# Splitting the attention burst between slots 8, 9 and 10, 11 of a fused retention and bilinear feed-forward kernel

## The chip, the cores and the metric

One core of a Trainium2 chip runs the whole program in one launch. The metric is the device time in microseconds (us). The engines are named as in the profile: PE (TensorE, its weight loads as PEld), DVE (VectorE), ACT (ScalarE), POOL (GpSimd) and SP (SyncE, which here issues all DMAs).

## The reference

A recurrent linear attention with a decay for each head feeds a bilinear feed-forward layer:

```python
# q, k, v: [4 batches, 8 heads, 768 steps, 64]
for t in range(S):
    state = gamma[None, :, None, None] * state + np.einsum('bhd,bhe->bhde', k[:, :, t], v[:, :, t])
    y[:, :, t] = scale * np.einsum('bhd,bhde->bhe', q[:, :, t], state)
x = y.transpose(0, 2, 1, 3).reshape(3072, 512)
out = ((x @ w_a) * (x @ w_b)) @ w_out        # w_a, w_b: 512 x 1536, w_out: 1536 x 512
```

## The kernel before

**Slots.** The 3072 tokens are cut into 24 slots of 128 tokens, six to a batch; slots 6 to 11 are the second batch. Two neighbouring slots form a pair. For each slot, q and k are multiplied by tables of the decay and cast to bf16 (`scaled`, tile `kqb`), then turned so that the head dimension lies on partitions (`kqT`). For the first three pairs the turning is done by PE (`flip2`: transposes into a PSUM tile `tp`, then one copy by ACT for k and one by DVE for q). For all later slots it is a DMA transpose, which `casts(t)` issues on SP right after POOL has made `kqb`; behind it, still in `casts(t)`, SP issues the loads of slot t+2.

**Attention of a slot.** `scores` multiplies k by q into two PSUM tiles `at` (32 small matmuls, line 261) and DVE multiplies them by a causal mask into `aT` (line 267). `update` adds k times v to the running state `st` in PSUM (8 matmuls, line 278) and copies it to `gst`, on the engine that it is given. `inter` multiplies q by `gst` (line 298) and `intra` multiplies `aT` by v (line 308), both into `ys`; `leave` copies `ys` to `xt`, the input of the feed-forward layer, on ACT.

**Bursts.** `turn(new, old, eng)` puts these together: scores and updates of the pair that begins at slot `new`, then `inter`, `intra` and `leave` of the pair that begins at `old`; either may be `None`. For `new` = 10 the last slot of the batch needs no update, so `turn` makes one update alone, that of slot 10: behind `inter` where there is an old pair, ahead of the scores where there is none.

**Feed-forward.** The slots are taken in eight groups J of `TILES` = 4, 2, 2, 2, 2, 4, 4, 4 slots. Group 2 holds slots 6 and 7, group 3 slots 8 and 9. `ffn_ab(J, ft)` is one of twelve steps of a group: four matmuls `a` (line 449), a cast of them by ACT (line 452), four matmuls `g` (line 459), and a product of both by DVE into `ht` (line 461). In groups 1 to 4 a matmul has 256 columns, in the others 512. The product with w_out is made for group 0 directly (`ffn_out`), for the others by a scheme of seven products of half matrices (`Group`, line 546) that uses sums of parts of `ht` (tiles `hs`, `hsum` and `hsums`, made by POOL for groups 2 to 4). `single(J, ...)` mixes these seven products with the first three steps of the next group.

**PSUM.** The eight banks are `ff` (three, in turn for `a`, `g`, `o`, `tp` and, with `scores(t, True)`, the two `at` tiles of one slot), `at0`, `at1`, `y0`, `y1` (one each) and `st`.

**Order.** Nothing is reordered on an engine: `seq` chains every instruction to the one before it on its engine, so the order of the calls at the end of the kernel (lines 620 to 794) is the order on every engine and on SP's queue. The part around the change:

```python
    turn(8, None)          # line 728: scores of 8 and 9, and their updates
    blocks(2, 7, 9)
    hsums(2, 0, 3, G_)
    casts(12)
    blocks(2, 9, 10)
    turn(10, 8, V_)        # line 733
    blocks(2, 10, NFT)
    hsums(2, 3, 6, G_)
    casts(13)
    single(2, Y0, AT0, FF)
    casts(14)
    blocks(3, 3, 6)
```

Of the kernel before, what the change touches and what calls it, by code (L numbers as in the profile page):

```python
# [10 lines left out]
BF16 = mybir.dt.bfloat16  # L11
# [12 lines left out]
def kernel(  # L24
# [11 lines left out]
    P = 128  # L36
    B, H, S, D = q.shape
    NCH = S // P
    HP = H // 2
# [24 lines left out]
    psff = ctx.enter_context(tc.tile_pool(name="psff", bufs=3, space=bass.MemoryType.PSUM))  # L64
    psat = ctx.enter_context(tc.tile_pool(name="psat", bufs=1, space=bass.MemoryType.PSUM))
# [6 lines left out]
    def seq(bi):  # L72
        ins = bi.ins
        prev = last.get(ins.engine)
        if prev is not None:
            tc.add_manual_dep(ins, prev.name, nosync, reason="program order")
        last[ins.engine] = ins
        return bi
# [114 lines left out]
    def cast(engine, dst, src):  # L193
        if engine is nc.scalar:
            seq(nc.scalar.copy(dst, src))
        else:
            seq(engine.tensor_copy(dst, src))  # L197
# [38 lines left out]
    def casts(t):  # L236
        new_nat(t)
        scaled(nc.gpsimd, t, 0)
        scaled(nc.gpsimd, t, 1)
        if t not in range(12, 20):  # L240
            cast(nc.gpsimd, vb[t], raws["v", t])
        if t % 2 == 0:
            kqT[t // 2] = tra.tile([P, 2, 2, HP, P], BF16, tag="kqT", name="kqT", bufs=3)
        seq(nc.sync.dma_start_transpose(
            out=kqT[t // 2][:, t % 2].rearrange("p a b c -> p (a b) c"),
            in_=kqb[t].rearrange("p a hp r d -> p (a hp r d)")))
        if t + 2 < NSLOT:
            load_slot(t + 2)
# [4 lines left out]
    def scores(t, ff):  # L253
        if ff:
            at = [psff.tile([P, HP, P], F32, tag="ff", name=f"at{r}") for r in range(2)]
        else:
            at = [psat.tile([P, HP, P], F32, tag=f"at{r}", name="at") for r in range(2)]
        for hp in range(HP):
            for c in range(2):
                for r in range(2):  # L260
                    seq(nc.tensor.matmul(at[r][half(c), hp, :],  # L261
                                         kqT[t // 2][half(r), t % 2, 0, hp, half(c)],
                                         kqT[t // 2][half(r), :, 1, hp, half(t % 2)],
                                         start=True, stop=True, skip_group_check=True))
        aT[t] = tra.tile([P, 2, HP, P], BF16, tag="aT", name="aT")
        for r in range(2):
            seq(nc.vector.tensor_tensor(aT[t][:, r], at[r], mask.to_broadcast([P, HP, P]), op=ALU.mult))  # L267

    def update(t, eng):
        ci = t % NCH  # L270
        if ci == NCH - 1:
            return
        if ci == 0:
            state[0] = psst.tile([P, HP, D], F32, tag="st", name="st")
        st = state[0]
        for hp in range(HP):
            for r in range(2):
                seq(nc.tensor.matmul(st[half(r), hp, :], kb[t][:, hp, r, :],  # L278
                                     vb[t][:, HP * r + hp, :],
                                     start=(ci == 0 and hp == 0), stop=(hp == HP - 1),  # L280
                                     skip_group_check=True))
        cast(eng, gst[(t + 1) % 4], st)
# [8 lines left out]
    def inter(t):  # L291
        if t % NCH == 0:
            return
        for j in range(2):
            for c in range(2):
                for r in range(2):
                    hp = 2 * j + c
                    seq(nc.tensor.matmul(ys[t // 2][r][half(c), j, :, t % 2, :],  # L298
                                         gst[t % 4][half(r), hp, :],
                                         kqT[t // 2][half(r), :, 1, hp, half(t % 2)],  # L300
                                         start=begin(t, c, r), stop=False, skip_group_check=True))

    def intra(t):
        for r in range(2):
            for j in range(2):
                for c in range(2):
                    hp = 2 * j + c
                    seq(nc.tensor.matmul(ys[t // 2][r][half(c), j, :, t % 2, :],  # L308
                                         vb[t][:, HP * r + hp, :], aT[t][:, r, hp, :],
                                         start=begin(t, c, r), stop=True, skip_group_check=True))  # L310

    def leave(t):
        J, i = where[t]
        if i == 0:
            xt[J] = xtp.tile([P, KT, 4 * P], BF16, tag="xt", name="xt")
        for r in range(2):
            seq(nc.scalar.copy(xt[J][:, 2 * r : 2 * r + 2, i * P : (i + 2) * P],  # L317
                               ys[t // 2][r].rearrange("p j a s n -> p j (a s n)")))

    def turn(new, old, eng=nc.scalar):  # L320
        if old is not None:
            ys[old // 2] = [psat.tile([P, 2, 2, 2, P // 2], F32, tag=f"y{r}", name="y") for r in range(2)]
        two = new is not None and (new + 1) % NCH < NCH - 1
        if new is not None:
            if two or old is None:
                update(new, eng)
            scores(new + 1, True)
            scores(new, False)
        if old is not None:
            inter(old)  # L330
            inter(old + 1)
        if two:
            update(new + 1, nc.scalar)
        elif new is not None and old is not None:
            update(new, eng)
        if old is not None:
            intra(old)
            intra(old + 1)
            leave(old)
# [9 lines left out]
        for t in (2 * u, 2 * u + 1):  # L349
            cast(nc.gpsimd, vb[t], raws["v", t])  # L350

    def flip2(u, i, on):
        if i == 0:
            kqT2[u] = tra.tile([P, 2, 2, HP, P], BF16, tag="kqT2", name="kqT2", bufs=2)
        for pars, eng in on:
            tp = psff.tile([P, 2, HP, P], BF16, tag="ff", name="tp")[:, : len(pars)]
            for n, par in enumerate(pars):
                for hp in range(HP):
                    seq(nc.tensor.transpose(tp[:, n, hp, :], kqb[2 * u + par][:, i, hp, :, :], ident))  # L359
            cast(eng, kqT2[u][:, pars[0] : pars[0] + len(pars), i], tp)  # L360
# [81 lines left out]
    def ffn_a(J, ft, c0=0, c1=None):  # L442
        c1 = TILES[J] * P if c1 is None else c1
        if J not in ht:
            ht[J] = htp.tile([P, NFT, 4 * P], BF16, tag="ht", name="ht")
        fs = slice(ft * P, (ft + 1) * P)
        a = psff.tile([P, 4 * P], F32, tag="ff", name="a")[:, : c1 - c0]
        for kt in range(KT):
            seq(nc.tensor.matmul(a, wa_bf[:, kt, fs], xcols(J, kt, c0, c1),  # L449
                                 start=(kt == 0), stop=(kt == KT - 1)))  # L450
        asb = asbs[J, ft, c0] = asbp.tile([P, 4 * P], BF16, tag="asb", name="asb")[:, : c1 - c0]
        seq(nc.scalar.copy(asb, a))  # L452

    def ffn_g(J, ft, c0=0, c1=None):
        c1 = TILES[J] * P if c1 is None else c1
        fs = slice(ft * P, (ft + 1) * P)
        g = psff.tile([P, 4 * P], F32, tag="ff", name="g")[:, : c1 - c0]
        for kt in range(KT):
            seq(nc.tensor.matmul(g, wb_bf[:, kt, fs], xcols(J, kt, c0, c1),  # L459
                                 start=(kt == 0), stop=(kt == KT - 1)))  # L460
        seq(nc.vector.tensor_tensor(ht[J][:, ft, c0:c1], g, asbs.pop((J, ft, c0)), op=ALU.mult))  # L461

    def ffn_ab(J, ft):
        store()
        ffn_a(J, ft)
        ffn_g(J, ft)
# [56 lines left out]
    def sums(J, ft):  # L523
        for what in WHEN.get(ft, []):
            hsum(J, *map(int, what))
# [94 lines left out]
    D_, G_, A_ = nc.vector, nc.gpsimd, nc.scalar  # L620
    K, Q = 0, 1
    warm(psat, "y1", 512, 512, 256)
    casts2(0, {(K, 1): D_, (K, 0): D_, (Q, 1): D_, (Q, 0): D_})
    flip2(0, K, [((0, 1), A_)])
    warm(psat, "y1", 128)
    flip2(0, Q, [((1,), D_)])
    flip2(0, Q, [((0,), D_)])
    warm(psat, "y1", 256)
    scores2(0, 1)
# [43 lines left out]
            scaled(D_, 5, Q)  # L673
    flip2(2, K, [((0, 1), A_)])
    ffn_a(0, 9)
    flip2(2, Q, [((0, 1), D_)])
    ffn_g(0, 9)
    scores2(2, 0, True)
    scores2(2, 1)
# [11 lines left out]
    V_ = nc.vector  # L691

    def blocks(J, a, b):
        for ft in range(a, b):
            ffn_ab(J, ft)
            if J >= 5:
                sums(J, ft)
# [32 lines left out]
    hsums(2, 0, 3, G_)  # L730
    casts(12)
    blocks(2, 9, 10)
    turn(10, 8, V_)
    blocks(2, 10, NFT)
    hsums(2, 3, 6, G_)
    casts(13)
    single(2, Y0, AT0, FF)
    casts(14)
    blocks(3, 3, 6)
    hsum(3, 3, 0, 6, G_)  # L740
    v_cast(12)
    blocks(3, 6, 8)
# [82 lines left out]
```

## Time and profile before

| | |
|---|---|
| time of the kernel, 3 runs | median 228.40 us (228.40 to 228.43) |
| the profiled execution | 228.36 us, its span 226.4 us, granted TensorE clock 0.998 |
| PE, DVE, ACT, POOL busy | 96%, 57%, 41%, 42% of the span |
| DMA | 39.67 MB, 74.4% of 16 engines |

In a timeline row the first number is the start, the second the duration, both in us from the start of the span; `[1.68 <-DMA x]` means that the engine stood idle for 1.68 us before the row until the DMA that writes x had landed. A PE row runs to the modelled end of its last matmul, which reaches into the next row: what a row costs in a full stream is the distance of the starts. In a row of waits stand the sum, the number of times and the longest.

### The profile page before, as it was taken

Reading aid. Unit: us, or ns where it says so; the run is one execution under the profiler, and the core shown is the slowest. Engines: PE = TensorE matmul, PEld = TensorE weight load, DVE = VectorE, ACT = ScalarE, POOL = GpSimd, SP = SyncE. Lnnn points to the kernel's source line nnn. Section 1 sums busy time; section 2 is a strip of 40 time slices with the busy share of each in tenths; the row PEclk is TensorE's granted clock in tenths of the full one; section 3 lists DMA queues with packets and bytes.
Section 4 is the critical chain, followed back from the end, with each engine's and each line's share of the span. In section 5 each row is a group of like instructions: output and inputs, shape, how many; then the busy total and the mean of one; then the engine's idle time right before and its main releaser. Section 6 shows DMA issues by size and latency. Waiting matters only on the chain.

```text
span 226.4 us, 5592 instructions
## 1 busy us (share of the span) xinstructions
PE 217.7 (96%) x2253; PEld 146.5 (65%) x2264; DVE 129.5 (57%) x255; ACT 91.9 (41%) x202; POOL 94.0 (42%) x111
## 2 busy tenths in 40 slices
PE   7899999999999969999999999999999999999993
PEld 3567445687468858888888555468654468444582
DVE  3785338646983565455476337993366563346732
ACT  3364334342243424464565355353343433333331
POOL 5365666677653767669629846600000000000000
PEclk9999999999999999999999999999999999999999
DMA  6999999999999997999897999920400000400005
GB/s 166 290 326 349 346 289 335 387 250 188 256 257 234 209 222 182 194 250 214 182 198 181 223 194 232 230 53 3 185 3 0 1 3 8 178 3 0 0 1 184
DMA packets 86904, 39.67 MB, mean 175 GB/s; under 512 B 57440, under 2 KB 82528, under 8 KB 86880
## 3 DMA queue, kind: packets, MB, share of 16 engines
q1 hardware_dynamic: 86880, 39.33, 74.4%
q8 instruction: 17, 0.28, 0.5%
q14 instruction: 7, 0.06, 0.1%
HBM read 28.31 MB, written 6.29 MB: 153 GB/s over the span
## 4 chain that ended last, share of the span: by engine, by line
PE 88%; DMA 6%; DVE 2%; SPq 2%; issue 1%; POOL 0%; DVEq 0%; POOLq 0%
PE g L459 27%; PE a L449 27%; PE mA L546 12%; PE mB L546 6%; PE o L480 5%; DMA qf<-in_q_dram 3%; PE mC L546 3%; DMA kqT<-kqb 2%; PE at L261 2%; PE y L308 2%; SPq L99 2%; PE st L278 1%; DVE kqb L229 1%; PE y L298 1%; PE y L414 1%; PE tp L359 1%
## 5 line engine op out<-in xcount | busy, mean ns | idle before, releaser
L461 DVE TENSOR_TENSOR ht<-g,asb 128x256 bf16<-128x256 f32 (+1 forms) x98 | 53.7, 549 | 55.6 <-PE g L459 50.8
L459 PE MATMUL g<-xt,wb_bf 128*128 128x256 bf16 (+1 forms) x392 | 77.8, 322 | 0.1
L449 PE MATMUL a<-xt,wa_bf 128*128 128x256 bf16 (+1 forms) x383 | 77.4, 321 | 0.5
L452 ACT CAST asb<-a 128x256 bf16<-128x256 f32 (+1 forms) x98 | 46.3, 473 | 67.1 <-PE a L449 64.7
L459 PEld LDWEIGHTS <-wb_bf 128*128 128x128 bf16 x392 | 38.2, 98 | 24.0
L449 PEld LDWEIGHTS <-wa_bf 128*128 128x128 bf16 x392 | 37.3, 98 | 22.4 <-issue 0.4
L229 POOL TENSOR_TENSOR kqb<-kf,ktab 128x512 bf16<-128x512 f32 x22 | 23.3, 1064 | 15.5 <-DMA kf<-in_k_dram 15.3
L546 PEld LDWEIGHTS <-hs 128*128 128x128 bf16 x240 | 23.5, 98 | 3.4
L267 DVE TENSOR_TENSOR aT<-at,mask 128x512 bf16<-128x512 f32 x36 | 22.3, 683 | 1.9 <-PE at L261 1.6
L229 POOL TENSOR_TENSOR kqb<-qf,qtab 128x512 bf16<-128x512 f32 x18 | 19.0, 1053 | 3.9 <-DMA qf<-in_q_dram 3.9
L552 ACT COPY snaps<-mA 128x256 f32<-128x256 f32 x30 | 11.2, 373 | 23.0 <-PE mA L546 23.0
L546 PEld LDWEIGHTS <-ht 128*128 128x128 bf16 x180 | 17.5, 98 | 2.7
L490 DVE TENSOR_TENSOR osb<-mB,snaps 128x256 f32<-128x256 f32 x20 | 8.5, 425 | 14.4 <-PE mB L546 7.1
L546 PE MATMUL mA<-wsum,hs 128*128 128x256 bf16 x120 | 15.9, 273 | 0.0
L197 POOL CAST vb<-vf 128x512 bf16<-128x512 f32 x16 | 10.5, 669 | 8.8 <-DMA vf<-in_v_dram 8.4
L490 POOL TENSOR_TENSOR hs<-ht,hs 128x384 bf16<-128x384 bf16 x12 | 10.9, 911 | 7.8 <-DVE ht L461 7.8
L490 POOL TENSOR_TENSOR hs<-ht 128x384 bf16<-128x384 bf16 (+1 forms) x9 | 10.4, 1153 | 6.4 <-DVE ht L461 6.4
L317 ACT CAST xt<-y 128x512 bf16<-128x512 f32 x18 | 9.7, 589 | 4.4 <-PE y L308 4.3
L490 DVE TENSOR_TENSOR osb<-mC,snaps 128x256 f32<-128x256 f32 x10 | 4.2, 422 | 12.2 <-ACT snaps L552 6.2
L480 PE MATMUL o<-wo_bf,ht 128*128 128x512 bf16 x46 | 10.6, 379 | 0.1
L490 DVE TENSOR_TENSOR hs<-ht,hs 128x512 bf16<-128x512 bf16 (+1 forms) x20 | 9.9, 496 | 0.2
L435 PE MATMUL idle<-zero 128*128 128x256 f32 (+2 forms) x16 | 8.2, 631 | 1.6 <-DVE zero L132 1.5
(64 smaller groups left out, 189.5 us busy)
## 6 DMA issues: line engine op xcount, KB each, us to landing
qf<-in_q_dram SPq DMA_DIRECT2D x12, 512.0 KB, 5.3
out_dram<-osb SPq DMA_DIRECT2D x22, 256.0 KB, 3.9
kf<-in_k_dram SPq DMA_DIRECT2D x18, 256.0 KB, 3.9
vf<-in_v_dram SPq DMA_DIRECT2D x18, 256.0 KB, 5.3
wsta<-in_moe_w_a_dram SPq DMA_DIRECT2D x6, 512.0 KB, 8.3
wstb<-in_moe_w_b_dram SPq DMA_DIRECT2D x6, 512.0 KB, 8.0
wsto<-in_moe_w_out_dram SPq DMA_DIRECT2D x6, 512.0 KB, 7.7
kf<-in_k_dram SPq DMA_DIRECT2D x3, 512.0 KB, 7.1
```

Source lines behind the costliest of these rows:

```text
L197: seq(engine.tensor_copy(dst, src))
L229: seq(eng.tensor_tensor(dst, src, tab, op=ALU.mult))
L267: seq(nc.vector.tensor_tensor(aT[t][:, r], at[r], mask.to_broadcast([P, HP, P]), op=ALU.mult))
L317: seq(nc.scalar.copy(xt[J][:, 2 * r : 2 * r + 2, i * P : (i + 2) * P], ys[t // 2][r].rearrange("p j a s n -> p j (a s n)")))
L449: seq(nc.tensor.matmul(a, wa_bf[:, kt, fs], xcols(J, kt, c0, c1), start=(kt == 0), stop=(kt == KT - 1)))
L452: seq(nc.scalar.copy(asb, a))
L459: seq(nc.tensor.matmul(g, wb_bf[:, kt, fs], xcols(J, kt, c0, c1), start=(kt == 0), stop=(kt == KT - 1)))
L461: seq(nc.vector.tensor_tensor(ht[J][:, ft, c0:c1], g, asbs.pop((J, ft, c0)), op=ALU.mult))
L480: seq(nc.tensor.matmul(o, ht[J][:, ft, i * P : (i + 1) * P], wo_bf[:, ft], start=(ft == 0), stop=(ft == NFT - 1)))
L490: seq(eng.tensor_tensor(dst, x, y, op=op))
L546: seq(nc.tensor.matmul(m, w, right[:, j], start=(first and j == 0), stop=(j == NP - 1), skip_group_check=True))
L552: seq(nc.scalar.copy(self.snaps[:, n], self.bank["A"]))
```

## The change

The call `turn(10, 8, V_)` becomes two. At its old place `turn(None, 8)` makes only `inter`, `intra` and `leave` of slots 8 and 9. Behind `single(2)`, `casts(14)` and one step of group 3, `turn(10, None, V_)` makes the update of slot 10 (with its copy of the state on DVE) and the scores of slots 11 and 10. Besides, the PE transposes of the third pair's q are written to bank `y0` instead of a bank of `ff`.

```diff
-    def flip2(u, i, on):
+    def flip2(u, i, on, pool=psff, tag="ff"):
...
-            tp = psff.tile([P, 2, HP, P], BF16, tag="ff", name="tp")[:, : len(pars)]
+            tp = pool.tile([P, 2, HP, P], BF16, tag=tag, name="tp")[:, : len(pars)]
...
     ffn_a(0, 9)
-    flip2(2, Q, [((0, 1), D_)])
+    flip2(2, Q, [((0, 1), D_)], psat, "y0")
     ffn_g(0, 9)
...
     blocks(2, 9, 10)
-    turn(10, 8, V_)
+    turn(None, 8)
     blocks(2, 10, NFT)
     hsums(2, 3, 6, G_)
     casts(13)
     single(2, Y0, AT0, FF)
     casts(14)
-    blocks(3, 3, 6)
+    blocks(3, 3, 4)
+    turn(10, None, V_)
+    blocks(3, 4, 6)
```

## The prediction

> **What bounds the kernel now.** I read the page first, then the waits of PE, the chain of waits around the longest of them, and timelines by engine of the places that the diff touches.
>
> ```profile
> span 226.4 us, 5592 instructions
> PE 217.7 (96%) x2253; PEld 146.5 (65%) x2264; DVE 129.5 (57%) x255; ACT 91.9 (41%) x202; POOL 94.0 (42%) x111
> ...
> PE at L261 <- DMA kqT<-kqb: 1.7, 1, 1.7
> PE tp L359 <- DVE ht L461: 0.5, 1, 0.5
> ...
> 77.71 5.58 DMA kqT<-kqb
> ```
>
> PE sets the end: it is busy for 96% of the span, and every other engine for 57% or less. PE's long waits on others behind the start-up are the two shown (page, waits of PE): 1.7 us for a DMA transpose and 0.5 us for DVE. The third view, the chain, names the transpose: issued at 77.71, landed 5.58 us later. Time is won or lost only where PE stands idle. The time is 228.36 us in this execution, the span and 1.96 us around it; the median of the runs, 228.40, is 0.04 above. I sum against the execution. About 0.2% (0.46 us) is what a measurement can tell from no change.
>
> **Edit 1, the old place.**
>
> ```profile
> 81.05 0.60 PE L459 MATMUL g<-xt,wb_bf 128*128 128x256 bf16 x4
> 83.33 0.64 PE L261 MATMUL at<-kqT 64*64 64x128 bf16 x32 [1.68 <-DMA kqT<-kqb]
> 83.80 0.39 PE L298 MATMUL y<-kqT,gst 64*64 64x128 bf16 x16
> ...
> 84.82 0.61 PE L449 MATMUL a<-xt,wa_bf 128*128 128x256 bf16 x4
> ...
> 94.30 0.60 PE L459 MATMUL g<-xt,wb_bf 128*128 128x256 bf16 x4
> 94.73 0.60 PE L449 MATMUL a<-xt,wa_bf 128*128 128x256 bf16 x4
> ...
> 176.62 1.03 PE L459 MATMUL g<-xt,wb_bf 128*128 128x512 bf16 x4
> ...
> 178.49 1.04 PE L449 MATMUL a<-xt,wa_bf 128*128 128x512 bf16 x3
> ...
> 180.39 0.86 PE a L449 x4
> ```
>
> Four matmuls of 256 columns take 0.44 us from start to start (94.30 to 94.73). So after `g` at 81.05 PE is free at 81.49, and the next feed-forward matmul comes at 84.82: `turn(10, 8)` costs 3.33 us, of which 1.68 are the wait for slot 11's transpose and the rest scores, `inter`, update and `intra`. What stays there is `turn(None, 8)`. The kernel has one such call alone, `turn(None, 22)`: its `g` starts at 176.62 and takes 0.86 (the row of four 512-column matmuls), so PE is free at 177.48 and goes on at 178.49: 1.01 us. Neither `gst` of slots 8 and 9 nor their `aT` are late (their masks end at 80.66, below). So the old place gets 3.33 - 1.01 = **2.32 us** shorter. The wait does not come back later with the scores: that transpose landed at 83.29, and they now come after 92.
>
> **Edit 1, the new place.** No row of before shows a score burst without `inter` and `intra` of an older pair beside it, but for `turn(8, None)`, which is my template.
>
> ```profile
> 76.94 0.60 PE L459 MATMUL g<-xt,wb_bf 128*128 128x256 bf16 x4
> 77.47 0.32 PE L278 MATMUL st<-vb,kqb 128*64 128x64 bf16 x8
> 77.72 0.64 PE L261 MATMUL at<-kqT 64*64 64x128 bf16 x32
> ...
> 77.65 0.42 DVE L461 TENSOR_TENSOR ht<-g,asb 128x256 bf16<-128x256 f32 x1 [0.45 <-PE g L459]
> 78.18 2.48 DVE L267 TENSOR_TENSOR aT<-at,mask 128x512 bf16<-128x512 f32 x4
> 80.58 0.75 DVE L461 TENSOR_TENSOR ht<-g,asb 128x256 bf16<-128x256 f32 x2
> ...
> 86.19 0.41 DVE L197 CAST gst<-st 128x256 bf16<-128x256 f32 x1
> 86.52 0.82 DVE L461 TENSOR_TENSOR ht<-g,asb 128x256 bf16<-128x256 f32 x2
> ...
> 96.92 0.60 PE L459 MATMUL g<-xt,wb_bf 128*128 128x256 bf16 x4
> ...
> L267 DVE TENSOR_TENSOR aT<-at,mask 128x512 bf16<-128x512 f32 x36 | 22.3, 683 | 1.9 <-PE at L261 1.6
> ```
>
> Call T the start of the update's matmuls, 0.09 us after PE is free (76.94 + 0.44 = 77.38, then 77.47). PE itself has little to do: 0.25 for the update (77.47 to 77.72), about 0.48 for 32 score matmuls (83.33 to 83.80), and could start the next `a` at T + 0.73. But DVE is in order, and behind its waits queue: the last `ht` at T + 0.18 (77.65 against 77.47), the copy of the state 0.35 later (second `ht` of a pair: 80.58 to 80.93), four masks 0.33 later (86.19 to 86.52) that follow each other every 0.60 (78.18 to 80.58 for four), and then the `ht` of the step behind the burst. That one starts at T + 0.18 + 0.35 + 0.33 + 2.40 = T + 3.26 and ends 0.41 later. PE waits for it: of the three `ff` banks one holds that step's `g` until then, one the next `g` and one the next `a`, so PE can run five sets of four (T + 0.73 + 5 x 0.44 = T + 2.93) and no further before T + 3.67 and 0.06 for the signal. The template shows both: its first `ht` of 80.58 ends at about 80.99, and its sixth set starts at 81.05. So the sixth set, `g` of step 5 counted from 1 (ft = 6), starts at T + 3.73, or 0.09 + 3.73 = 3.82 after PE was free; before, it started 96.92 - 94.73 = 2.19 after. The burst costs **1.63 us** here. DVE has caught up after that (each set of two takes 0.87 on PE and 0.42 on DVE). Bounds: without the copy in the chain 1.63 - 0.33 = 1.3; with no overlap of the DVE instructions (a mask at the 683 ns of its group instead of 0.60, the copy at 0.41, the `ht` at 0.42) about 0.5 more, 2.1.
>
> The turn is moved past three `hs` sums and four `kqb` products on POOL, and past two transposes, the loads of slots 15 and 16 and two stores on SP. It issues nothing on either queue itself, so their order stays; on ACT it has nothing at the new place either. Net of edit 1: 2.32 - 1.63 = **0.69 us** gained.
>
> The cover of what comes 2.3 us earlier in between is POOL's sums for `single(2)`:
>
> ```profile
> 87.43 0.91 POOL L490 TENSOR_TENSOR hs<-ht,hs 128x384 bf16<-128x384 bf16 x1 [1.31 <-DVE ht L461]
> ...
> 89.49 0.82 PE L546 MATMUL mA<-wsum,hs 128*128 128x256 bf16 x6
> ```
>
> POOL was idle for 1.31 us before the second half of sum 2, so it can start at 86.12 and end at 87.03. PE needs that half for the fourth of the six matmuls, 0.33 after 89.49 - 2.32 = 87.17, that is 87.50. It holds by 0.47 us; each 0.1 that POOL is later than that would cost PE 0.1.
>
> **Edit 2, the transposes of q.**
>
> ```profile
> 35.42 0.68 DVE L461 TENSOR_TENSOR ht<-g,asb 128x512 bf16<-128x512 f32 x1
> ...
> 36.16 0.61 PE L359 MATMUL tp<-ident,kqb 128*128 128x128 bf16 x8 [0.49 <-DVE ht L461]
> 36.60 1.03 PE L459 MATMUL g<-xt,wb_bf 128*128 128x512 bf16 x4
> ...
> 37.22 1.04 POOL L197 CAST wa_bf<-wsta 128x1024 bf16<-128x1024 f32 x1 [0.30 <-DMA wsta<-in_moe_w_a_dram]
> 38.34 2.47 DVE L377 TENSOR_TENSOR aT<-at,mask 128x512 bf16<-128x512 f32 x4
> 38.48 1.02 PE L449 MATMUL a<-xt,wa_bf 128*128 128x512 bf16 x4
> ...
> 39.50 0.58 PE y L414 x16
> 41.50 0.35 PE y L414 x16
> ```
>
> The transposes waited for an `ff` bank that DVE freed with the `ht` ending at 36.10. Bank `y0` was last read by the copies of the second pair, which stand ahead of group 0's steps in the order of the calls; it is free. So the transposes start about 0.6 earlier, and `g` behind them can take the bank freed at 36.10, at 36.16 instead of 36.60: 0.44 earlier. What is late next is `a` at 38.48: its weights are cast by POOL, after a DMA, until 38.26, so it gains 0.05 or so. But DVE, which got its `g` and its q earlier, does the masks 0.44 earlier, and the first `intra` no longer waits for the second mask: the same 16 matmuls take 0.58 at 39.50 and 0.35 at 41.50. I take 0.05 + 0.23 = **0.28 us**; ends 0.05 (the `intra` waits as before) and 0.49 (all of the wait).
>
> Sum: 228.36 - 0.69 - 0.28 = 227.39, **227.4 us**.
>
> **What is late next.** After 100 us PE runs 0.97 earlier, and the nearest transposes are those of slot 17:
>
> ```profile
> 111.87 1.19 SPq L94 DMA_DIRECT2D vf<-in_v_dram  x1
> 113.16 2.54 SPq L244 DMA_TRANSPOSE kqT<-kqb  x1
> ...
> DMA to landing us min/median/max: 6.2/6.2/6.2
> ...
> 119.84 0.73 PE L261 MATMUL at<-kqT 64*64 64x128 bf16 x32
> ...
> 99.94 0.91 POOL L490 TENSOR_TENSOR hs<-ht,hs 128x384 bf16<-128x384 bf16 x1 [1.04 <-DVE ht L461]
> ...
> DMA to landing us min/median/max: 3.0/4.5/6.2
> ```
>
> (The first landing line is that issue's own, the second that of all 18.) Landed at 119.36, used at 119.84: 0.48 to spare. The products on POOL that lead there follow without a pause from the sum at 99.94, which waits for DVE's `ht` and so for PE; they come earlier with it, and the 0.48 stays. The Trainium skill ("DMA: Bandwidth & Descriptors", section "Queues, rings and completion order") states that each DMA engine takes descriptors in the order of its ring; by that rule this transpose stands behind the loads issued up to 111.87 and can come earlier only with them, and were they fixed, PE would wait 0.49 at 118.87 and the time would be 227.9. The 6.2 here against 3.0 at the least agrees with the rule; that the loads move with POOL is what decides, and no run here shows it yet.
>
> **Rivals.**
> - *A. The burst alone costs what the wait cost (no change).* DVE's instructions do not overlap (+0.5), and the second score tile is given the bank of the last `g`, so that the scores wait for its `ht` at T + 0.65 instead of T + 0.25 (+0.4). 227.39 + 0.9 = 228.3. Against it: in the template neither happened. 0.15.
> - *B. More.* The copy of the state falls out of DVE's chain (-0.33) or all of the 0.49 is won (-0.21): down to 226.9. Against: the copy stands ahead of the masks on the same engine. 0.13.
> - *C. Slower: the wait moves to slot 17's transposes.* They need not be removed from the chain, only late: if they land after 118.87, PE waits, and if after 119.84, the kernel is slower than before. Were the issue as much earlier as PE and the landing 1.7 longer (the spread from the median 4.5 to 6.2), they land at 113.16 - 0.97 + 7.9 = 120.1, 1.2 late: 228.6; with the issue not moved as well, 229.6. Against: nothing is added to SP's queue, and 6.2 is already the longest of 18. 0.12.
> - *D. The change doesn't do what it says:* `y0` is not free, or `g` gets a bank that is freed later; edit 2 gives nothing, 227.7. This lies within my range of edit 2.
>
> **How the numbers follow.** The forecast with D has 0.60, its own range 227.1 to 228.0 (bounds of both edits, 0.3 to 1.2 gained, nearly added up). A 0.15, B 0.13, C 0.12. Faster by over 0.2% is the forecast but for its slow end and B: 0.57 + 0.13 = 0.70; within 0.2% the most of A and that end: 0.16; slower C and a rest of A: 0.14. The range 227.0 to 228.5 leaves out the far end of B and most of C.
>
> **What would show it.** Right: the wait of 1.7 us is gone from PE's waits; `a` after the old place 2.3 us earlier than 84.82 (with 0.3 more of edit 2); `at` of slots 11 and 10 near 92.3, behind one step of group 3; then PE idle for 0.8 us in the next five sets, ended by DVE's `aT` and `ht`; sets at 100 us 0.9 to 1.0 earlier; `tp` without its 0.49. Wrong: PE waiting for `hs` in `single(2)`, for `kqT` near 119, or the sixth set later than T + 4.3.

## The result and the profile after

The changed kernel takes 227.52 us (median of 5 runs, 227.38 to 227.58) against 228.43 (228.40 to 228.66) for the kernel before in the same comparison: ratio 0.9956, 95% interval 0.9942 to 0.9971. It is 0.9 us faster. The profiled execution took 227.52 us. A ratio here and below leaves out executions that took over 1.5% longer than the fastest of the same kernel; the medians keep them.

The page of the changed kernel, its span and the busy time by engine:

```profile
span 225.4 us, 5593 instructions
PE 218.2 (97%) x2253; PEld 146.2 (65%) x2264; DVE 128.9 (57%) x255; ACT 91.9 (41%) x202; POOL 94.2 (42%) x111
```

Its waits of PE behind the start-up (sum, times, longest, in us):

```profile
...
PE a L449 <- POOL wa_bf L197: 0.3, 1, 0.3
PE g L459 <- DVE aT L267: 0.2, 1, 0.2
```

The wait of 1.7 us for the transpose and the 0.5 us of `tp` for `ht` are gone. In their place stand two short ones: 0.3 for a weight cast by POOL behind edit 2, and 0.2 for the masks behind the moved scores. A list of waits does not show all that a burst costs, though; the starts of the rows do. The timelines of the changed kernel, PE at the four places in question, then DVE, ACT and POOL, SP's queue, and PE again at the scores of slot 17:

```profile
35.53 0.61 PE L359 MATMUL tp<-ident,kqb 128*128 128x128 bf16 x8
36.18 1.02 PE L459 MATMUL g<-xt,wb_bf 128*128 128x512 bf16 x4
...
38.31 1.04 PE L449 MATMUL a<-xt,wa_bf 128*128 128x512 bf16 x4 [0.29 <-POOL wa_bf L197]
39.28 0.42 PE L414 MATMUL y<-aT,vb 64*64 64x128 bf16 x16
39.63 0.62 PE L403 MATMUL y<-kqT,gbd 128*128 128x128 bf16 x8
...
80.67 0.60 PE L459 MATMUL g<-xt,wb_bf 128*128 128x256 bf16 x4
...
82.11 0.61 PE L449 MATMUL a<-xt,wa_bf 128*128 128x256 bf16 x4
...
86.78 0.82 PE L546 MATMUL mA<-wsum,hs 128*128 128x256 bf16 x6
...
91.59 0.60 PE L459 MATMUL g<-xt,wb_bf 128*128 128x256 bf16 x4
92.12 0.32 PE L278 MATMUL st<-vb,kqb 128*64 128x64 bf16 x8
92.36 0.64 PE L261 MATMUL at<-kqT 64*64 64x128 bf16 x32
92.93 0.61 PE L449 MATMUL a<-xt,wa_bf 128*128 128x256 bf16 x4
93.70 0.60 PE L459 MATMUL g<-xt,wb_bf 128*128 128x256 bf16 x4 [0.15 <-DVE aT L267]
...
95.35 0.60 PE L449 MATMUL a<-xt,wa_bf 128*128 128x256 bf16 x4
95.82 0.60 PE L459 MATMUL g<-xt,wb_bf 128*128 128x256 bf16 x4
96.41 0.60 PE L449 MATMUL a<-xt,wa_bf 128*128 128x256 bf16 x4
...
99.12 0.32 PE L278 MATMUL st<-vb,kqb 128*64 128x64 bf16 x8
...
92.29 0.42 DVE L461 TENSOR_TENSOR ht<-g,asb 128x256 bf16<-128x256 f32 x1 [0.52 <-PE g L459]
92.63 0.41 DVE L197 CAST gst<-st 128x256 bf16<-128x256 f32 x1
92.97 2.47 DVE L267 TENSOR_TENSOR aT<-at,mask 128x512 bf16<-128x512 f32 x4
95.36 0.74 DVE L461 TENSOR_TENSOR ht<-g,asb 128x256 bf16<-128x256 f32 x2
...
94.93 0.37 ACT L452 CAST asb<-a 128x256 bf16<-128x256 f32 x1 [0.98 <-PE a L449]
...
95.99 0.37 ACT L452 CAST asb<-a 128x256 bf16<-128x256 f32 x1 [0.17 <-PE a L449]
...
85.69 0.91 POOL L490 TENSOR_TENSOR hs<-ht,hs 128x384 bf16<-128x384 bf16 x1
...
111.90 2.70 SPq L244 DMA_TRANSPOSE kqT<-kqb  x1
...
118.89 0.73 PE L261 MATMUL at<-kqT 64*64 64x128 bf16 x32
```

At the old place `a` follows 1.00 us after PE is free of `g` (80.67 + 0.44 = 81.11, then 82.11). At the new place T is 92.12, and the sixth set, `g` at 95.82, starts at T + 3.70. The next burst, which begins with the update of slot 12, starts at 99.12. In the kernel before, PE's timeline has it at 100.06:

```profile
100.06 0.32 PE L278 MATMUL st<-vb,kqb 128*64 128x64 bf16 x8
```

The 0.94 us between them are what the change is worth by the traces, and the medians differ by 0.91.

### The profile page after: what moved, and what is told of

Read it like the earlier page. It is cut to its first block, busy times and chain, and to the rows that moved or that the text cites. A ratio compares the mean times of both kernels' runs of the same rounds, so it can differ in the third digit from the quotient of the medians.

```text
span 225.4 us, 5593 instructions
## 1 busy us (share of the span) xinstructions
PE 218.2 (97%) x2253; PEld 146.2 (65%) x2264; DVE 128.9 (57%) x255; ACT 91.9 (41%) x202; POOL 94.2 (42%) x111
## 4 chain that ended last, share of the span: by engine, by line
PE 81%; DMA 11%; SPq 5%; POOL 1%; DVE 1%; issue 1%; DVEq 0%
PE a L449 24%; PE g L459 24%; PE mA L546 12%; DMA wstb<-in_moe_w_b_dram 8%; PE mB L546 6%; PE o L480 5%; SPq L99 3%; DMA wsta<-in_moe_w_a_dram 3%; PE mC L546 3%; PE at L261 2%; PE y L308 2%; PE st L278 2%; SPq L111 1%; PE y L298 1%; POOL wb_bf L197 0%
```

## Experiments

The ratios below come from three other chips, on which executions of the kernel before scattered more widely (228.13 to 233.17 us). They compare with the kernel before on the same chip, and medians are set beside each other only within one chip: the two edits alone, the copy on ACT and the split at once ran on one, the long and the filled wait on another, and the last four on a third.

**Each edit alone.** The first kernel keeps the split and drops the other bank; the second does the reverse.

```diff
-    flip2(2, Q, [((0, 1), D_)], psat, "y0")
+    flip2(2, Q, [((0, 1), D_)])
```

> Edit 1 alone: the turn is split, the transposes of q stay in an ff bank. Theory (the two edits act at separate places and add up): the old place is 2.3 us shorter, the new one costs 1.75 us, so 0.55 less than before, about 227.9 us; PE's wait of 0.5 us ahead of the transposes of q is there as before. Rival (the whole gain is the removed wait of 1.7 us less a small burst, and the bank does nothing): 227.5 us.

> Edit 2 alone: the transposes of q in bank y0, the turn unsplit. Theory: PE is 0.4 us earlier from 40 us on, but slot 11's transpose lands when it did, at about 83.3 to 83.5, so the wait at the old place grows from 1.7 to about 2.1 us and the gain is swallowed there: about 228.4 us, no change. Rival (the edits add up): 0.4 less, 228.0 us.

Measured: the split alone has a median of 227.85 us, ratio 0.993 (0.990 to 0.996); the bank alone has a median of 230.46 (228.16 to 232.38), ratio 1.0004 (0.9959 to 1.0049). PE's timeline of the split alone:

```profile
36.19 0.61 PE L359 MATMUL tp<-ident,kqb 128*128 128x128 bf16 x8 [0.49 <-DVE ht L461]
...
92.53 0.32 PE L278 MATMUL st<-vb,kqb 128*64 128x64 bf16 x8
...
96.24 0.60 PE L459 MATMUL g<-xt,wb_bf 128*128 128x256 bf16 x4
96.83 0.60 PE L449 MATMUL a<-xt,wa_bf 128*128 128x256 bf16 x4
```

The wait of `tp` is back, and the burst is the same: the sixth set at T + 3.71 and the next `a` 0.59 behind it. The median lies at the 227.9 us that was expected and not at the rival's 227.5; the ratio says more than the expected 0.55 us, and a part of that belongs to the scatter of the kernel before (see the long wait below). The bank alone, in PE's waits:

```profile
PE at L261 <- DMA kqT<-kqb: 3.3, 1, 3.3
```

PE reaches the scores earlier and waits longer, so that what edit 2 wins at 36 us is lost again at 83. That it is swallowed whole agrees with the theory but is not shown, because the interval is wider than the 0.3 us in dispute, and in this execution (231.73 us) the transpose was also issued later.

**What bounds the new place.** The copy of the state goes to ACT, so that it leaves DVE's queue ahead of the masks.

```diff
-    turn(10, None, V_)
+    turn(10, None, A_)
```

> Both edits, but the copy of slot 10's state at the new place is made by ACT instead of DVE. Theory (DVE's queue of ht, copy, four masks and ht sets the length of the burst): each instruction behind the copy starts 0.3 us earlier, the sixth set of matmuls starts at T + 3.4 instead of T + 3.7, and the time is 0.3 less, about 227.2 us. Rival (the banks that ACT frees, or the signals, bind as closely): T + 3.7 and 227.5 us.

Measured: median 227.32 us, ratio 0.9915 (0.9882 to 0.9948), 0.53 below the split alone, which lacks the other bank besides. The timelines of PE and DVE at the new place:

```profile
92.14 0.32 PE L278 MATMUL st<-vb,kqb 128*64 128x64 bf16 x8
...
95.72 0.60 PE L459 MATMUL g<-xt,wb_bf 128*128 128x256 bf16 x4
96.30 0.60 PE L449 MATMUL a<-xt,wa_bf 128*128 128x256 bf16 x4
...
92.85 2.48 DVE L267 TENSOR_TENSOR aT<-at,mask 128x512 bf16<-128x512 f32 x4
95.25 0.74 DVE L461 TENSOR_TENSOR ht<-g,asb 128x256 bf16<-128x256 f32 x2
```

The sixth set comes at T + 3.58, not T + 3.4. DVE's chain does set the burst: the masks come earlier by 0.14 against T (T + 0.71 instead of T + 0.85), and so do the `ht` and the sixth set, by 0.12 to 0.13. But the copy was worth only that: with it gone the masks come behind the scores themselves, which PE starts at T + 0.25. Two limits stood 0.14 apart, and taking one away showed the other.

**Later, or only apart?** Both calls are made at the old place, one behind the other.

```diff
     turn(None, 8)
+    turn(10, None, V_)
     blocks(2, 10, NFT)
...
-    blocks(3, 3, 4)
-    turn(10, None, V_)
-    blocks(3, 4, 6)
+    blocks(3, 3, 6)
```

> Both edits, but the second turn follows the first at once, at the old place. Theory (the distance to the transpose's landing is what gains, not the split): PE waits again about 1.1 to 1.3 us for slot 11's transpose ahead of the scores, and DVE's masks come behind it; the time is that of before, less at most 0.2, 228.2 to 228.5 us. Rival (the split itself, by making a shorter burst, gains): 227.5 to 227.8 us.

Measured: median 227.95 us, ratio 0.9941 (0.9905 to 0.9977), against 227.85 for the split alone and 227.32 with the copy on ACT on the same chip. The theory expected 228.2 to 228.5 and missed. `inter`, `intra` and the update of slot 10 now stand ahead of the wait and fill some 1.2 us of it (in the profile PE is free of `g` at 81.14 and the row of the update ends at 82.34); the theory did expect a shorter wait, of 1.1 to 1.3 us, but gave the time at most 0.2 for it. The rest of the wait stays, as PE's waits show:

```profile
PE at L261 <- DMA kqT<-kqb: 2.1, 1, 2.1
```

So part of what the edit brings at the old place comes from the new order of the parts alone. How much the distance adds can't be read from these medians: they differ little, and this profile (229.95 us) has a lower clock behind the wait, which is the next question. The eight executions of the split at once whose mean granted clock was 0.997 or more have a median span of 225.85 us, the eight with the copy on ACT, 0.12 of it due to the copy, one of 225.4. At full clock the distance therefore adds about 0.3 us, an estimate from these spans.

**What a long wait costs.** Windows of the split at once; the columns are the busy times of PE, PEld, DVE, ACT and POOL, then the granted clock, the DMA share and GB/s:

```profile
...
84.00:85.00 1.00, 0.58 (x24) 0.59 (x28) 0.00 (x0) 0.00 (x0) 1.00 (x2) 0.75 1.27 242
85.00:87.00 2.00, 2.00 (x28) 1.39 (x17) 1.94 (x4) 0.37 (x1) 0.76 (x1) 0.50 1.20 300
87.00:88.00 1.00, 1.00 (x7) 0.69 (x6) 0.87 (x2) 0.00 (x0) 0.00 (x0) 0.54 1.59 237
...
```

Behind the idle time of 2.08 us the clock is at half for about 3.4 us: a mean of 0.75 in the window from 84 to 85 puts the fall at 84.50, and one of 0.54 in that from 87 puts the rise at 87.92. Two kernels test whether the idle time does this. The first lengthens the wait of the kernel before; the second fills it with matmuls on zeros (the line with `warm`, which the first lacks).

```diff
+        if t == 11:
+            load_slot(13)
         seq(nc.sync.dma_start_transpose(
...
-        if t + 2 < NSLOT:
+        if t + 2 < NSLOT and t != 11:
...
+    warm(psat, "y1", *[512] * 12)
     turn(10, 8, V_)
```

> The kernel before, with slot 13's two loads issued ahead of slot 11's transpose instead of behind it, so that the transpose is issued about 1.6 us later (the two loads take 0.57 and 1.00 on SP) and the wait of 1.68 us becomes about 3.3. By the theory (an idle time of PE of 2 us or more is followed by some 3 us at a granted clock of 0.5, as in the profiles of the split at once, 2.08 us idle, and of the bank alone, 3.30 us) the time rises by the 1.6 and by half of about 3 us, to about 231.5, and the table of windows shows 0.5 behind the scores. By the rival (those two clocks fell because of the chip's own disturbance and not because of the idle time) it rises by the 1.6 alone, to about 230.0, and the clock stays near 1.0.

> The same, with 12 matmuls of 512 columns on zeros ahead of the scores (at about 0.21 us each 2.6 us of the wait are filled; their result is used by nothing). The transpose lands when it did, so PE is idle for 1 us or less instead of 3.3. By the theory the clock stays near 1.0 and the time is about 230.0, some 1.5 below the kernel without them, although PE does more work; by the rival it is the same as without them.

Measured: the long wait 233.35 us (232.79 to 234.57), ratio 1.0117 (1.0039 to 1.0195); the filled one 236.75 (236.71 to 236.91), ratio 1.0274 (1.0209 to 1.034). Both sizes were off. The wait became 5.17 us instead of 3.3, and the 12 matmuls of 512 columns took 10.46 us instead of 2.6, so that they overfilled it and the filled kernel is the slower one, where 1.5 us less had been expected. The scores behind the long wait in PE's timeline:

```profile
86.87 1.07 PE L263 MATMUL at<-kqT 64*64 64x128 bf16 x32 [5.17 <-DMA kqT<-kqb]
```

In its windows the granted clock is the number ahead of the last two:

```profile
85.00:86.00 1.00, 0.00 (x0) 0.00 (x0) 0.00 (x0) 0.00 (x0) 1.00 (x2) 0.86 1.42 127
...
92.00:93.00 1.00, 1.00 (x9) 0.79 (x7) 0.00 (x1) 0.37 (x1) 0.00 (x0) 0.73 1.02 242
```

PE's timeline of the filled wait:

```profile
81.56 10.46 PE L437 MATMUL idle<-zero 128*128 128x512 f32 x24
91.95 0.64 PE L263 MATMUL at<-kqT 64*64 64x128 bf16 x32
```

Its window:

```profile
82.00:92.00 10.00, 10.00 (x28) 4.22 (x30) 0.25 (x1) 0.00 (x0) 4.19 (x5) 1.00 1.25 223
```

With the wait idle the clock is at half from 85.72 to 92.54, 6.8 us or twice the 3.4. With the wait filled it is 1.00 over the whole window from 82 to 92. The filled kernel begins its scores 5.08 us later and is only 3.4 us slower by the medians (spans 235.0 and 232.8): about 1.7 of the delay, and 2.9 in the profiled pair, is won back by the full clock. The rival, that the clock fell by chance, would have left the two 5.1 apart. Nor is it only the profiled pair: the mean granted clock is 0.985 to 0.992 in all four executions of the idle kernel and 0.997 to 1.000 in all four of the filled one.

The other executions agree. By these lengths one stretch of 3.4 us at half clock lowers the mean over a span of 228 us by 0.007, two by 0.015 (an estimate). Of the 61 executions of the kernel before on these chips 25 have a mean of 0.993 or less, most of them 0.989 to 0.993 and two 0.984 and 0.985; so have 7 of 12 of the bank alone and 4 of 12 of the split at once, which wait for the transpose too. None of the 35 of the split alone, the copy on ACT and the last two kernels below has, and they do not wait there. So the ratios of about 0.99 on these chips hold more than the 0.9 us of the changed kernel's own comparison: part of them is half clock that the kernel before pays in some executions. That each of those had a longer wait is not shown, since only single executions were traced.

**Covering the burst.** If the bound at the new place is the PSUM banks that DVE empties, products that need none of those banks should hide it. In `single(2)` three products of 0.66 us each stand together, into `y0`, `at0` and one `ff` bank. The burst is put ahead of them, and the second product moves from `at0` to `y1`; a control leaves it in `at0`.

```diff
     blocks(2, 10, NFT)
+    turn(10, None, V_)
     hsums(2, 3, 6, G_)
...
-    single(2, Y0, AT0, FF)
+    single(2, Y0, Y1, FF)
...
-    blocks(3, 3, 4)
-    turn(10, None, V_)
-    blocks(3, 4, 6)
+    blocks(3, 3, 6)
```

> Both edits, but the second turn stands between the last step of group 2 and the seven products of group 2, whose second product takes bank y1 instead of at0. Theory (the burst costs PE time because the feed-forward steps behind it need the banks that DVE's queue frees one by one; three products, 2.0 us, that need none of them would cover it): slot 11's transpose has landed at 83.3 to 84.5 and is needed at 84.3; PE pays 0.25 + 0.48 us for its own matmuls and next to nothing more, 0.82 instead of 1.77 us: about 226.6 us, up to 0.4 more where the transpose lands late. Rival (DVE's 2.4 us of masks are paid wherever the burst stands): 227.5 us.

> As the run before, but the second product keeps bank at0, which the scores of slot 10 hold until DVE's third mask. Theory of banks: that product waits from T + 1.4 to T + 2.8, 1.4 us, and the time is 1.4 above the run with y1, about 228.0 us. Rival (the banks don't matter, the engines' work does): the same as the run with y1.

Measured: with `y1` a median of 227.13 us (226.38 to 230.38), ratio 0.9898 (0.9864 to 0.9931); with `at0` 228.55 (227.60 to 230.48), ratio 0.9983 (0.9949 to 1.0016). PE's timeline with `y1`:

```profile
83.56 0.60 PE L459 MATMUL g<-xt,wb_bf 128*128 128x256 bf16 x4
84.09 0.32 PE L278 MATMUL st<-vb,kqb 128*64 128x64 bf16 x8
...
84.91 0.83 PE L546 MATMUL mA<-wo_bf,ht 128*128 128x256 bf16 x6
...
```

PE's timeline with `at0`:

```profile
84.24 0.32 PE L278 MATMUL st<-vb,kqb 128*64 128x64 bf16 x8
...
87.02 0.81 PE L546 MATMUL mB<-wsum,hs 128*128 128x256 bf16 x6 [1.13 <-DVE aT L267]
```

With `y1` the burst costs PE's own work and the signal, 0.91 us (free at 83.56 + 0.44 = 84.00, the first product at 84.91), and nothing waits behind it. With one product in a bank that holds scores the wait is 1.13 us, at T + 2.78 as expected, and the medians are 1.4 apart. Banks, not PE's work, make the burst dear. The median with `y1` missed the expected 226.6 by 0.5 all the same. In its trace the update of slot 12 starts at 98.33, 0.79 earlier than in the changed kernel, but two of its nine executions took 228.31 and 230.38; in the trace the transpose lands 0.98 us before the scores start (77.85 + 5.5 = 83.35, then 84.33), and whether it came later in those two is not known.

**The steadier version.** The burst stands behind the second product inside `single(2)`, the product in `y1`, the copy on ACT.

```diff
-    def single(J, A, B, C):
+    def single(J, A, B, C, burst=None):
...
         g.p1()
         g.p7()
+        if burst:
+            burst()
         g.p2()
...
-    single(2, Y0, AT0, FF)
+    single(2, Y0, Y1, FF, lambda: turn(10, None, A_))
...
-    blocks(3, 3, 4)
-    turn(10, None, V_)
-    blocks(3, 4, 6)
+    blocks(3, 3, 6)
```

> Both edits, the second turn behind the second of the seven products of group 2 (which takes bank y1), 1.3 us later than in the run with y1, and the copy of the state on ACT. Theory: the transpose of slot 11 has landed in every execution; one product of 0.66 us covers the queue of DVE in part; PE waits at most 0.2 us: about 226.7 us, and the executions lie as close together as those of the changed kernel. Rival (covers don't help): 227.3 us, as with the copy on ACT alone.

Measured: median 226.95 us (226.60 to 227.25), ratio 0.9895 (0.986 to 0.9929).

PE's timeline:

```profile
98.50 0.32 PE L278 MATMUL st<-vb,kqb 128*64 128x64 bf16 x8
```

The update of slot 12 starts at 98.50, 0.62 earlier than in the changed kernel but 0.17 later than with the burst ahead of all three products (98.33). What this version has over that one is that its six executions lie close together, as expected; its median is 0.25 above the expected 226.7. It beats the kernel before and the changed one, though not by the whole 1% of its ratio: on the same chip it stands 0.60 below the kernel of the next experiment, whose time should be that of the changed one.

**What the transpose's landing depends on.** In the changed kernel the loads of slot 18 are issued behind slot 17's transpose instead of ahead of it.

```diff
-        if t + 2 < NSLOT:
+        if t == 17:
+            load_slot(18)
+        if t + 2 < NSLOT and t != 16:
             load_slot(t + 2)
```

> Both edits; the loads of slot 18 are issued behind slot 17's transpose instead of ahead of it. Theory (that transpose landed after 6.2 to 6.4 us because it stands behind 1 MB of loads in SP's queue): it lands 3.0 to 4.5 us after its issue, some 3 us or more before PE needs it; nothing waits for the loads of slot 18, so the time stays, 227.5 us. Rival (the landing time is set by something else on the DMA engines): 5.5 us or more.

Measured: median 227.55 us, ratio 0.9917 (0.9888 to 0.9946). The answer for line 244 and slot 17, the length of the issue on SP's queue in ns and the landing:

```profile
L244 SPq DMA_TRANSPOSE kqT<-kqb x1: 1233/1233/1233, 111.3 to 111.3; - x1
DMA to landing us min/median/max: 5.0/5.0/5.0
```

The changed kernel's own answer for slot 17, where the issue took 2.70 us (its row of 111.90 above):

```profile
DMA to landing us min/median/max: 6.4/6.4/6.4
```

It landed after 5.0 us instead of 6.4, between the two expectations. The landing is counted from the start of the issue, and the 1.4 us are the issue's own: 2.70 us right behind the three loads, 1.23 without them. Behind the end of the issue the transpose took 3.7 us with the loads ahead of it and 3.8 without. Slot 16's transpose, with an issue of the same 1.23 us in the same trace, landed after 3.1; what the other 1.9 us of slot 17 are stays open.

## Why the prediction was right, step by step

**The sum** of 0.97 us in the span was seen as 0.94 (100.06 to 99.12), and 227.4 us as 227.52. Two of its terms were off by 0.1 each and cancelled; that the sum came out so close is luck to that extent.

- **Edit 1, the old place.** Forecast 2.32. The `a` behind it came 2.71 earlier (84.82 to 82.11); 0.38 of that is edit 2, seen at the `g` ahead (81.05 to 80.67). That leaves 2.33. The template `turn(None, 22)` gave the right cost, 1.01 against 1.00.
- **Edit 1, the new place.** Forecast 1.63, measured 1.76. The chain of DVE came as written: `ht` at T + 0.17, copy at T + 0.51, masks from T + 0.85, `ht` at T + 3.24, sixth set at T + 3.70. The failed step is the sentence that DVE "has caught up after that". The set behind the sixth starts 0.59 later instead of 0.44, at 96.41, which is 4.38 after PE was free at 92.03, where a free stream takes 2.62 (2.19 and 0.43). DVE is idle by then. It starts 0.05 behind the end of ACT's cast of the `a` of 95.35 (95.99 to 96.36), as that `a` itself starts 0.05 behind the cast of the one before it (94.93 to 95.30). So while DVE held two of the banks, the third went from one `a` to the next, each time through PE and ACT. That this is the cause is argued from these times; the lag of 0.58 to 0.59 is in all four profiles with the burst at this place, and no run tried it by itself. The template could not show it: its sixth set, at 81.05, is the last before the old burst.
- **The cover by POOL.** The idle 1.31 us went; the second half of the sum ran from 85.69 to 86.60, and PE needed it at 86.78 + 0.33 = 87.11. It held by 0.51, forecast 0.47.
- **Net of edit 1:** 2.33 - 1.76 = 0.57 instead of 0.69.
- **Edit 2.** Forecast 0.28, measured 0.38 at the `g` of 80.67; the third experiment agrees, which has 0.41 over the split alone beyond the 0.12 of the copy (0.53 in the medians). The transposes came 0.63 earlier and `g` 0.42; the first `intra` took 0.35 instead of 0.58, as forecast. Mis-sized was the gain at `a`: 0.05 was allowed because POOL's cast ends at 38.26, and 0.17 came (38.48 to 38.31). The distance of 0.22 between cast and `a` in the kernel before was no signal time but PE's own work; the signal takes 0.05.
- **What is late next.** The loads moved with POOL, as the forecast needed: the last one ahead of slot 17's transpose from 111.87 to 110.92, and the issue behind it from 113.16 to 111.90. POOL's products do not follow without a pause, as the prediction has it: in the kernel before POOL stood idle for 0.67 us ahead of the one at 109.87, until the load of k had landed. Slot 17's transpose landed after 6.4 us, at 118.30, with 0.59 to spare before PE's scores at 118.89 (forecast 0.48). The Trainium skill's rule in "DMA: Bandwidth & Descriptors", section "Queues, rings and completion order", is that descriptors are taken in ring order. The run with three loads (1 MB) issued behind the transpose neither needs nor refutes it: the 1.4 us that the landing lost are the shorter issue, and with the loads ahead or not it took 3.7 or 3.8 us from there. So the reading that 6.2 against 3.0 agrees with the rule was too quick.
- **The rivals.** A: the scores started at T + 0.24 and the masks followed each other without extra time, so neither half of its price was paid. B: the copy did not fall out of the chain by itself; made to, it brought 0.12 and not 0.33. The prediction's own template had that: no copy stands ahead of its masks on DVE, and they start at T + 0.71 and its sixth set at T + 3.58 (78.18 and 81.05 with T at 77.47), the times that the copy on ACT gave. Of the 0.49 at `tp`, 0.38 were won. C: the wait did not return at slot 17. D: `y0` was free.

## What to carry to other kernels

A burst into PSUM that DVE must empty costs PE more than its own matmuls: 1.76 us here for 0.73 of work, because the sets behind it wait in turn for the banks. Before such a burst is moved away from a wait, look for neighbours that write to banks outside of it; three products of 0.66 us hid what separation alone did not. And in a chain of times, a distance between a producer's end and a consumer's start is a signal time only if the consumer was idle.

## What the runs showed of the hardware

PE's idle time of 1.68 us in the kernel before left the granted clock at 1.00. Idle times of 2.08 us (the split at once), 3.30 (the bank alone) and 5.17 (the long wait) were followed by half clock for 3.42, 3.40 and 6.82 us. It began 0.08 us after PE had taken up work again in the first, 1.04 after in the second (at 85.68, by a mean of 0.84 in the window from 85) and before it in the third. The Trainium skill ("TensorE: Matmul & The Clock Gate", section "What's actually happening") ties half clock to at least one idle window of about 3.4 us, with windows that run free of the kernel. The lengths, one and two times 3.4, agree; the idle time needed does not, since 2.08 us were enough here.

SP's issue of a slot's transpose took 1.23 to 3.12 us in the changed kernel. Of the seven issued from 78 to 112 us, four took 1.23 to 1.77 and landed 3.2 to 4.0 us after their start; three took 2.47 to 3.12 and landed after 5.1 to 6.4.
